# Row maxima of a banded attention: the mask moves from VectorE's add-and-max into a product on TensorE

## The chip, the cores and the metric

The kernel runs on one core of one Trainium2 chip. The metric is device time of one execution in microseconds (us), the lower the better. The median of three runs of the kernel before is 436.84 us (435.81 to 437.22).

## The reference

Three layers follow each other. The first is attention over 4 batches of 8 heads, 576 positions, head size 64, with a causal window of 128 positions and a linear bias for each head:

```python
scores = scale * np.matmul(q, k.transpose(0, 1, 3, 2))
bias = slopes[:, None, None] * (-np.abs(rel).astype(np.float32))[None, :, :]
mask = (rel >= 0) & (rel < window)
scores = np.where(mask, scores + bias[None], -1000000000.0)
scores = scores - np.max(scores, axis=-1, keepdims=True)
attn = np.exp(scores)
attn = attn / (np.sum(attn, axis=-1, keepdims=True) + 1e-09)
return np.matmul(attn, v).astype(np.float32)
```

The second is a soft mixture of 8 experts on the 2304 x 512 result (logits against `phi`, softmax over tokens to fill 32 slots, two expert products, softmax over slots to read them back). The third is a feed-forward layer, 512 to 2048 to 512, with a leaky maximum between. All of it is float32. The change touches the row maximum of the first layer alone.

## The kernel before

The first part of the kernel, up to about 160 us, is a software pipeline over the 32 heads (`g`). Each head is cut into steps with a letter each (table `UNITS`), each letter has a due time in units of heads (table `XO`), and all steps of all heads are sorted by head number plus due time and written out in that order. Engines work through their own instructions strictly in the order in which they are written, so this table sets which step stands before which on each engine; the change doesn't touch it.

The steps that matter here, for one head:

- TQ and TK: TensorE transposes q and k (L266, three instructions each, tile `tp`). HQ and HK: ScalarE rounds them into `qb` and `kb` (L279). LQ and LK: VectorE takes what the rounding left over into `kq` (L284, L286, two instructions each). DQ and DK: GpSimd copies into the other half of `kq` (L292).
- A, B, C (function `smax`): TensorE computes the scores that the row maximum is taken of, into PSUM tiles `sm`, of which there are two. The 576 rows are five tiles of 128 (the last of 64). A row tile needs the columns of its own tile and of the one before: 256, 128 for the first tile, 192 for the last. A makes tiles 0 and 1, C tiles 2 and 3, B tile 4; B stands before A. One product for a tile (L306).
- XA, XB, XC (function `smax_v`): VectorE adds the band mask `maskt` to a tile and takes the maximum of each row, in one custom instruction for a tile (L316), which also writes the sum to a scratch tile `junk`; a short second instruction then writes the maximum to a column of `mn`.
- M, MS, DM: TensorE transposes `mn` (L325), ScalarE copies it (L330, tile `ms`), and a DMA puts it as one more row into `qb` (L333), so that the next score product subtracts the maximum.
- S and s (L351, L352, tile `st`): the scores proper: two products for each of five key blocks; E0, E1: ScalarE's exponential (L359); G0, G1: GpSimd sets to zero what lies outside the band (L367 to L377); P, Q: TensorE multiplies with v (L416, 32 small products, tile `o_ps`); N1, N2, N3: VectorE divides by the row sum (L431, L433, L437).

After each eight heads a batch is complete, and its part of the mixture layer (L460 to L639: transposes, logits, maxima, slot sums) is slotted between the heads that follow. The weights of the experts stream in through SyncE's DMA queue all the while. From about 173 us on TensorE runs through the experts and the feed-forward layer almost without a break.

Set-up work stands ahead of the pipeline: GpSimd builds `maskt` from a memset with two selections (L212 to L214), after that it fills rows of `qb` and `kb` (L224, L226).

Of the kernel before, what the change touches and what calls it, by code (L numbers as in the profile page):

```python
# [13 lines left out]
ALU = mybir.AluOpType  # L14
AX = mybir.AxisListType
# [6 lines left out]
def attn_softmoe_ffn(ctx: ExitStack, tc: tile.TileContext, q, k, v, phi, w1, w2, w_in, w_out, cst_in, out):  # L22
    nc = tc.nc
    B, H, S, D = q.shape
# [32 lines left out]
    NEG = -1.0e30  # L57
# [9 lines left out]
    small = ctx.enter_context(tc.tile_pool(name="small", bufs=4))  # L67

    ident = const.tile([128, 128], F32, name="ident")
# [24 lines left out]
    def view(nm, w=None, o=0):  # L94
        w = dict(sizes)[nm] - o if w is None else w
        return ar[:, off[nm] + o:off[nm] + o + w]

    def slot(nm, dt=F32):
        if nm[0] == "a":
            t = ar[:, SLOT * int(nm[1:]):SLOT * int(nm[1:]) + SLOT]  # L100
            return t if dt == F32 else t.bitcast(dt)
        return pools[nm[0]].tile([128, SLOT], dt, tag=nm, name=nm)

    maskt = view("maskt", 256)
    units_w = [(0, g, kc, h) for h in range(2) for g in range(E // 4) for kc in range(KD)]
    units_w += [(1, g, fc, 0) for h in range(2) for g in range(E // 4) for fc in range(4 * h, 4 * h + 4)]
    W = {u: [None] * 4 for u in units_w}
# [6 lines left out]
    def put_w(i, j0, t):  # L114
        n = t.shape[1] // 512
        for j in range(n):
            W[units_w[i]][j0 + j] = t[:, 512 * j:512 * j + 512]
        return t.rearrange("p (e f) -> p e f", e=n), src_w(i, j0, j0 + n)

    with tc.manual_schedule():  # L120
# [17 lines left out]
        mn = [at.tile([128, 5], F32, name=f"mn{i}") for i in range(2)]  # L138
# [58 lines left out]
        o, i, _, _ = bulk.pop()  # L197
# [11 lines left out]
        nc.vector.memset(bm4, 1.0)  # L209
        nc.gpsimd.affine_select(out=bm4, in_=bm4, pattern=[[-32, 4], [0, 16]], compare_op=ALU.is_ge, fill=0.0, base=0, channel_multiplier=1)  # L210
        nc.gpsimd.affine_select(out=bm4, in_=bm4, pattern=[[32, 4], [0, 16]], compare_op=ALU.is_ge, fill=0.0, base=31, channel_multiplier=-1)
        nc.vector.memset(maskt, 0.0)  # L212
        nc.gpsimd.affine_select(out=maskt, in_=maskt, pattern=[[-1, 256]], compare_op=ALU.is_ge, fill=NEG, base=128, channel_multiplier=1)
        nc.gpsimd.affine_select(out=maskt, in_=maskt, pattern=[[1, 256]], compare_op=ALU.is_gt, fill=NEG, base=0, channel_multiplier=-1)  # L214
        nc.vector.reduce_sum(out=cn[:, 0, 0, :], in_=ident.rearrange("p (i c) -> p c i", c=32), axis=AX.X)
        nc.vector.tensor_copy(blk.bitcast(F32R).rearrange("p (i c) -> p i c", c=32), cn[:, 0, 0:1, :].to_broadcast([128, 4, 32]))
        nc.vector.memset(lsb[64:128, 4, :], NEG)
# [18 lines left out]
        for i in range(NP):  # L236
            t = slot(f"p{i}")
# [57 lines left out]
        sms = {}  # L295

        def smax(part):
            def f(g):
                K1, Q1 = kb[g % R], qb[g % R]
                tl = ps.tile([128, 512], F32, tag="sm", name="sm", bufs=5 - TPB)  # L300
                o, jobs = 0, []
                for t in ((0, 1), (2, 3), (4,))[part]:
                    c0, c1 = max(0, 128 * t - 128), min(S, 128 * t + 128)
                    n, mr = c1 - c0, min(128, S - 128 * t)
                    sl = tl[0:mr, o:o + n]
                    nc.tensor.matmul(sl, lhsT=Q1[:, 128 * t:128 * t + mr], rhs=K1[:, c0:c1], start=True, stop=True)  # L306
                    jobs.append((t, sl, c0 - (128 * t - 128), n, mr))
                    o += n
                sms[part, g] = jobs
            return f  # L310

        def smax_v(part):
            def f(g):
                for t, sl, m0, n, mr in sms.pop((part, g)):
                    jk = small.tile([128, 256], mybir.dt.bfloat16, tag="junk", name="junk", bufs=2)
                    nc.vector.tensor_tensor_reduce(  # L316
                        out=jk[0:mr, 0:n], in0=sl, in1=maskt[0:mr, m0:m0 + n], op0=ALU.add, op1=ALU.max,
                        accum_out=mn[g % 2][0:mr, t:t + 1], scale=1.0, scalar=NEG)
            return f

        mss = {}
# [511 lines left out]
        for h in range(2):  # L833
            pp = ps.tile([128, 512], F32, tag=f"pb{h}", name="pb")
            for g in range(2):
                for kc in range(KD):
                    t = W.pop((0, g, kc, h))
                    for j in range(4):
                        nc.tensor.matmul(pp[32 * j:32 * j + 32, :], lhsT=siT[:, g, kc, :], rhs=t[j],  # L839
                                         start=(g == kc == 0), stop=(g == 1 and kc == KD - 1), tile_position=(0, 32 * j))  # L840
                    if (h, g, kc) == (0, 0, 2):
                        p = ps.tile([128, 2], F32, tag="pa", name="pa")
# [7 lines left out]
        i, j = divmod(late + NL, 4)  # L850
        k = 0
        while i < len(units_w):
            if i == len(units_w) - PRE:
                load_wi(0, "p8")
            o, src = put_w(i, j, slot(f"p{k}")[:, 0:512 * (4 - j)])
            nc.sync.dma_start(out=o, in_=src)
            i, j, k = i + 1, 0, k + 1
# [29 lines left out]
        for i in range(2 * FC):  # L887
            _, g, fc, _ = u = units_w[2 * FC + i]
            t = W.pop(u)
            for j in range(4):  # L890
                nc.tensor.matmul(p2[32 * j:32 * j + 32, :], lhsT=hT[:, g, fc, :], rhs=t[j],  # L891
                                 start=(i == 0), stop=(i == 2 * FC - 1), tile_position=(0, 32 * j))
# [85 lines left out]
        base = 0  # L978
        for j, (t0, n, f0, f1) in enumerate(visits):
# [3 lines left out]
            base = (base + 3 * (n // TB)) % 6  # L983
# [67 lines left out]
        for n, u in enumerate(units):  # L1051
            o = n + min(1.9 + .13 * n, ZO["O"])
# [99 lines left out]
```

## Time and profile before

| what | value |
|---|---|
| median of three runs | 436.84 us |
| span of the profiled execution | 434.6 us |
| TensorE products, busy | 419.8 us, 97%, 3480 instructions |
| VectorE, busy | 284.1 us, 65%, 894 instructions |
| ScalarE, busy | 239.0 us, 55% |
| GpSimd, busy | 140.5 us, 32% |
| L316, the add-and-max (160) | 53.6 us on VectorE, 374 ns each |
| L306, its score products (160) | 34.6 us on TensorE, 310 ns each |

The profile shows one execution. The end of a product on TensorE is modelled and products overlap, so a busy share of 97% doesn't say that TensorE has no room; how far apart the starts of products stand says more, and most of the rows below are read that way. A share of the whole span also hides that VectorE is nearly always busy in the first 153 us and idle most of the time after 240 us. [...]

### The profile page before, as it was taken

The numbers are of one execution on the slowest core, as the hardware profiler recorded it, in microseconds if no ns is written. First come the engines' busy times: TensorE is split into PE (matmuls) and PEld (weight loads), VectorE is DVE, ScalarE is ACT, GpSimd is POOL, SyncE is SP. The second block draws the span as 40 slices with busy tenths as digits, with TensorE's granted clock in tenths as the row PEclk, the third lists the DMA queues.
The fourth block names the chain that finished last, engine by engine and source line by source line (L and its number), as shares of the span: only waits on it lengthen the run. The fifth ranks groups of instructions, "written<-read, shape, count | busy, mean of one in ns | idle before, by whom it ended". The sixth has DMA issues, their size and how long they took to land.

```text
span 434.6 us, 9853 instructions
## 1 busy us (share of the span) xinstructions
PE 419.8 (97%) x3480; PEld 338.2 (78%) x3480; DVE 284.1 (65%) x894; ACT 239.0 (55%) x555; POOL 140.5 (32%) x331
## 2 busy tenths in 40 slices
PE   7898999999999999999999999999999999999996
PEld 6797889888788886333877888788878888888885
DVE  7898899999999964112999885767552233225242
ACT  4586777677678733021886765555554344344440
POOL 6497788687778845020000002020202000000000
PEclk9999999999999999999999999999999999999999
DMA  7768777778867979999987005000000003004012
GB/s 163 222 185 230 227 221 215 219 207 243 229 197 220 261 254 391 321 407 413 411 305 245 31 2 193 2 1 0 2 0 0 2 9 137 0 0 148 0 74 72
DMA packets 66801, 70.15 MB, mean 161 GB/s; under 512 B 23168, under 2 KB 42016, under 8 KB 66752
## 3 DMA queue, kind: packets, MB, share of 16 engines
q1 hardware_dynamic: 66304, 69.24, 49.5%
q8 instruction: 28, 0.46, 0.4%
q10 hardware_dynamic: 448, 0.28, 0.2%
q14 instruction: 21, 0.17, 0.1%
HBM read 64.70 MB, written 4.72 MB: 160 GB/s over the span
## 4 chain that ended last, share of the span: by engine, by line
PE 84%; DVE 6%; DMA 5%; issue 2%; POOL 1%; ACT 1%; DVEq 0%; SPq 0%; POOLq 0%; ACTq 0%
PE acc L1015 45%; PE o_ps L416 6%; PE ph L992 4%; PE sm L306 4%; PE pb L839 3%; PE pb L891 3%; PE st L352 3%; PE st L351 3%; PE tp L266 3%; DMA qb<-ms 2%; DMA ar<-in_q_dram 2%; DVE kq L284 1%; DMA ar<-in_k_dram 1%; PE tp L460 1%; PE tp L482 1%
## 5 line engine op out<-in xcount | busy, mean ns | idle before, releaser
L1015 PE MATMUL acc<-p,p 128*128 128x512 f32 x648 | 158.7, 390 | 0.0
L1015 PEld LDWEIGHTS acc<-p,p 128*128 128x128 f32 x648 | 120.7, 188 | 24.5 <-issue 1.7
L1005 DVE TENSOR_TENSOR p<-ar,p 128x384 fp32r<-128x384 f32 x96 | 52.9, 556 | 89.6 <-ACT ar L1001 89.4
L997 ACT ACTIVATE p<-ph 128x384 fp32r<-128x384 f32 (+1 forms) x97 | 47.5, 491 | 92.4 <-PE ph L992 92.4
L316 DVE CUSTOM_DVE_ANT_0 junk<-sm,ar 128x256 bf16<-128x256 f32 (+2 forms) x160 | 53.6, 374 | 4.5 <-PE sm L306 4.1
L1015 PE MATMUL acc<-b,p 128*128 128x512 f32 x216 | 53.6, 392 | 0.0
L785 POOL TENSOR_TENSOR p<-ar,p 128x512 fp32r<-128x512 f32 x8 | 10.6, 1329 | 124.9 <-ACT p L785 108.7
L359 ACT ACTIVATE ar<-st 128x512 f32<-128x512 f32 x64 | 38.3, 599 | 17.2 <-PE st L352 9.8
L1001 ACT ACTIVATE ar<-ph 128x384 f32<-128x384 f32 x96 | 47.1, 490 | 0.0
L1015 PEld LDWEIGHTS acc<-b,p 128*128 128x128 f32 x216 | 40.1, 188 | 8.2 <-DVE ql L1030 0.4
L416 PE MATMUL o_ps<-ar 128*64 128x65 f32 x992 | 41.3, 227 | 0.0
L416 PEld LDWEIGHTS o_ps<-ar 128*64 128x64 f32 x992 | 36.5, 137 | 4.7 <-issue 1.0
L351 PE MATMUL st<-kq 128*128 128x256 f32 (+1 forms) x160 | 39.7, 277 | 0.0
L352 PE MATMUL st<-qb,kb 128*128 128x256 f32 (+1 forms) x160 | 35.7, 270 | 2.1 <-DMA qb<-ms 2.1
L306 PE MATMUL sm<-kb,qb 128*128 128x256 f32 (+2 forms) x160 | 34.6, 310 | 2.6 <-DVE mn L316 1.0
L279 ACT ACTIVATE qb<-tp 64x288 fp32r<-64x288 f32 x64 | 28.0, 437 | 14.0 <-PE tp L266 13.2
L992 PE MATMUL ph<-p,p 128*128 128x384 f32 x96 | 33.1, 350 | 0.0
L266 PE MATMUL tp<-ident,ar 96*128 96x96 f32 x192 | 28.5, 258 | 2.3 <-DMA ar<-in_q_dram 1.4
L352 PEld LDWEIGHTS st<-qb,kb 128*128 128x128 f32 (+1 forms) x160 | 28.6, 179 | 2.5 <-DMA qb<-ms 2.5
L284 DVE SCALAR_TENSOR_TENSOR kq<-tp,qb 64x288 fp32r<-64x288 f32 x64 | 29.2, 457 | 1.9
L279 ACT ACTIVATE kb<-tp 64x288 fp32r<-64x288 f32 x64 | 28.0, 437 | 4.4 <-PE tp L266 3.0
L286 DVE TENSOR_TENSOR kq<-tp,kb 64x288 fp32r<-64x288 f32 x64 | 29.1, 454 | 1.7
(204 smaller groups left out, 618.0 us busy)
## 6 DMA issues: line engine op xcount, KB each, us to landing
p<-in_moe_w_dram SPq DMA_DIRECT2D x56, 256.0 KB
p<-in_moe_w_dram SPq DMA_DIRECT2D x7, 1024.0 KB
p<-in_moe_w_in_dram SPq DMA_DIRECT2D x5, 1024.0 KB
p<-in_moe_w_out_dram SPq DMA_DIRECT2D x5, 1024.0 KB
ar<-in_q_dram SPq DMA_DIRECT2D x32, 144.0 KB
ar<-in_k_dram SPq DMA_DIRECT2D x31, 144.0 KB
out_dram<-ar SPq DMA_DIRECT2D x17, 256.0 KB
ar<-in_v_dram SPq DMA_DIRECT2D x32, 128.0 KB
```

The source lines that it names most:

```text
L266: nc.tensor.transpose(p[:, 96 * u:96 * u + 96], n[:, 128 * u:128 * u + 128], ident[0:96, 0:96])
L279: nc.scalar.activation(out=b1, in_=pr, func=AF.Copy, scale=2.0 ** (g % H - 2) if half else 1.0)
L306: nc.tensor.matmul(sl, lhsT=Q1[:, 128 * t:128 * t + mr], rhs=K1[:, c0:c1], start=True, stop=True)
L316: nc.vector.tensor_tensor_reduce(out=jk[0:mr, 0:n], in0=sl, in1=maskt[0:mr, m0:m0 + n], op0=ALU.add, op1=ALU.max, accum_out=mn[g % 2][0:mr ...
L351: nc.tensor.matmul(sl, lhsT=KX[:, k0:k1], rhs=QA[:, q0:q1], start=True, stop=False)
L352: nc.tensor.matmul(sl, lhsT=kb[g % R][:, k0:k1], rhs=qb[g % R][:, q0:q1], start=False, stop=True)
L416: nc.tensor.matmul(o_ps[64 * u:64 * u + 64, t, :], lhsT=lt, rhs=r, start=st, stop=sp, tile_position=(0, 64 * u))
L992: nc.tensor.matmul(p, lhsT=mst[:, 128 * f:128 * f + 128], rhs=rhs, start=True, stop=True)
L997: nc.scalar.activation(out=G[t0, f][0][:, c], in_=H1[t0, f][:, c], func=AF.Prelu, alpha=0.01)
L1001: nc.scalar.activation(out=gg, in_=H1.pop((t0, f)), func=AF.Prelu, alpha=0.01)
L1005: nc.vector.tensor_tensor(out=g2, in0=G0.pop((t0, f)), in1=g1.bitcast(F32), op=ALU.subtract)
L1015: nc.tensor.matmul(acc[t0][t], lhsT=(g1, g1, g2)[k][:, 128 * t:128 * t + 128], rhs=(WO1, WO2, WO1)[k][c][:, i], start=(f == f0 and k == 0) ...
```

## The change

The mask becomes a bfloat16 tile of 320 columns, and a bfloat16 copy `idb` of the unit matrix stands beside it in the same place in SBUF. In `smax`, each score product is preceded by a product of `idb` with a piece of the mask into the same piece of PSUM; the score product then adds onto it. The tiles are grouped anew: A makes tiles 1 and 2, C tiles 3 and 4, both 256 columns wide (tile 4 is now taken with 128 rows, of which 64 are padding, and 256 columns), and B makes tile 0 with 128 columns. In `smax_v`, VectorE takes the plain maximum (`reduce_max`) of both tiles of A in one instruction, the same for C, and of the one tile of B. The scratch tile `junk` is gone.

```diff
-    maskt = view("maskt", 256)
+    BF16 = mybir.dt.bfloat16
+    maskt = view("maskt", 160).bitcast(BF16)
+    idb = view("maskt", 64, 160).bitcast(BF16)
...
+        nc.vector.tensor_copy(idb, ident)
         nc.vector.memset(maskt, 0.0)
-        nc.gpsimd.affine_select(out=maskt, in_=maskt, pattern=[[-1, 256]], compare_op=ALU.is_ge, fill=NEG, base=128, channel_multiplier=1)
-        nc.gpsimd.affine_select(out=maskt, in_=maskt, pattern=[[1, 256]], compare_op=ALU.is_gt, fill=NEG, base=0, channel_multiplier=-1)
+        nc.gpsimd.affine_select(out=maskt, in_=maskt, pattern=[[-1, 320]], compare_op=ALU.is_ge, fill=NEG, base=192, channel_multiplier=1)
+        nc.gpsimd.affine_select(out=maskt, in_=maskt, pattern=[[1, 320]], compare_op=ALU.is_gt, fill=NEG, base=-64, channel_multiplier=-1)
...
-                for t in ((0, 1), (2, 3), (4,))[part]:
-                    c0, c1 = max(0, 128 * t - 128), min(S, 128 * t + 128)
-                    n, mr = c1 - c0, min(128, S - 128 * t)
-                    sl = tl[0:mr, o:o + n]
-                    nc.tensor.matmul(sl, lhsT=Q1[:, 128 * t:128 * t + mr], rhs=K1[:, c0:c1], start=True, stop=True)
+                ts = ((1, 2), (3, 4), (0,))[part]
+                w = 256 if part < 2 else 128
+                for i, t in enumerate(ts):
+                    c1 = min(S, 128 * t + 128)
+                    m0 = 64 + 256 - w + c1 - (128 * t + 128)
+                    nc.tensor.matmul(tl[:, w * i:w * i + w], lhsT=idb, rhs=maskt[:, m0:m0 + w], start=True, stop=False)
+                    nc.tensor.matmul(tl[:, w * i:w * i + w], lhsT=Q1[:, 128 * t:128 * t + 128], rhs=K1[:, c1 - w:c1], start=False, stop=True)
...
-                for t, sl, m0, n, mr in sms.pop((part, g)):
-                    jk = small.tile([128, 256], mybir.dt.bfloat16, tag="junk", name="junk", bufs=2)
-                    nc.vector.tensor_tensor_reduce(
-                        out=jk[0:mr, 0:n], in0=sl, in1=maskt[0:mr, m0:m0 + n], op0=ALU.add, op1=ALU.max,
-                        accum_out=mn[g % 2][0:mr, t:t + 1], scale=1.0, scalar=NEG)
+                t, sl = sms.pop((part, g))
+                nc.vector.reduce_max(out=mn[g % 2][:, t:t + sl.shape[1]], in_=sl, axis=AX.X)
```

On TensorE, the stretch of one head from the end of its products with v (`o_ps`) to the start of the scores proper (`st`) holds the maxima's transpose and then B and A. Before:

```order
L416 MATMUL o_ps<-ar 64x65 x16
L325 MATMUL tp<-ident,mn_98 5x128
L306 MATMUL sm<-kb_94,qb_95 64x192
L306 MATMUL sm<-kb_94,qb_95 128x128
L306 MATMUL sm<-kb_94,qb_95 128x256
L351 MATMUL st<-kq_90 128x256
```

The same place now (lines are a few numbers off; `ar` is the place in SBUF that holds `idb` and the mask, and the loading of `idb` has a row of its own):

```order
L415 MATMUL o_ps<-ar 64x65 x16
L324 MATMUL tp<-ident,mn_98 5x128
L309 LDWEIGHTS ar
L309 MATMUL sm<-ar 128x128
L310 MATMUL sm<-kb_94,qb_95 128x128
L309 LDWEIGHTS ar
```

Three score products of 192, 128 and 256 columns have become six products, of 128, 128 and four times 256 columns; C, a little later, goes from two products of 256 columns to four.

On VectorE, the stretch of one head from the division of a head's result (N1: L431) to the leftover of the next q (LQ: L284) holds XB, XA and XC. Before:

```order
L431 TENSOR_SCALAR rs<-o_ps 128x5
L316 ISA junk,mn_98<-sm,ar 64x192
L316 ISA mn_98 64x1
L433 RECIPROCAL rs<-rs 128x5
L437 TENSOR_TENSOR ar<-o_ps,rs 128x5x64
L316 ISA junk,mn_98<-sm,ar 128x128
L316 ISA mn_98 128x1
L316 ISA junk,mn_98<-sm,ar 128x256
```

After the last row its short second instruction follows, and then the same pair twice more, for C. The same place now:

```order
L430 TENSOR_SCALAR rs<-o_ps 128x5
L317 TENSOR_REDUCE mn_98<-sm 128x1
L432 RECIPROCAL rs<-rs 128x5
L436 TENSOR_TENSOR ar<-o_ps,rs 128x5x64
L317 TENSOR_REDUCE mn_98<-sm 128x2 x2
L287 SCALAR_TENSOR_TENSOR kq_96<-tp,qb_95 64x288 x2
```

Ten instructions of a head have become three; their places among the others are the same, and what follows them is the same.

## Rows read from the trace of the kernel before

**Rows 1.** Stretch: length, busy PE, PEld, DVE, ACT, POOL (instructions), clock, DMA share, GB/s
```profile
59.45:97.69 38.24, 37.03 (x520) 32.63 (x518) 36.15 (x153) 28.02 (x69) 29.83 (x74) 1.00 0.77 216
```

**Rows 2.** VectorE in order of time, one head: start, us, engine, line, operation, shapes
```profile
91.53 0.49 DVE L437 TENSOR_TENSOR ar<-o_ps,rs 128x320 f32<-128x320 f32 x1
91.94 0.28 DVE L316 CUSTOM_DVE_ANT_0 junk<-sm,ar 128x128 bf16<-128x128 f32 x1
...
92.14 0.42 DVE L316 CUSTOM_DVE_ANT_0 junk<-sm,ar 128x256 bf16<-128x256 f32 x1
...
93.29 0.95 DVE L284 SCALAR_TENSOR_TENSOR kq<-tp,qb 64x288 fp32r<-64x288 f32 x2
...
95.33 0.34 DVE L316 CUSTOM_DVE_ANT_0 junk<-sm,ar 64x192 bf16<-64x192 f32 x1
...
95.60 0.17 DVE L433 RECIPROCAL rs<-rs 128x5 f32<-128x5 f32 x1
95.81 0.49 DVE L437 TENSOR_TENSOR ar<-o_ps,rs 128x320 f32<-128x320 f32 x1
```

**Rows 3.** TensorE in order of time, one head with batch work, 117.96 to 122.61 us
```profile
117.96 0.27 PE L325 MATMUL tp<-ident,mn 128*5 128x128 f32 x1
117.99 0.58 PE L306 MATMUL sm<-kb,qb 128*64 128x192 f32 x3
118.41 0.28 PE L351 MATMUL st<-kq 128*128 128x256 f32 x1
118.53 0.28 PE L352 MATMUL st<-qb,kb 128*128 128x256 f32 x1
...
118.89 0.28 PE L630 MATMUL tp<-col,dn 128*128 128x2 f32 x2
...
119.42 0.36 PE L351 MATMUL st<-kq 128*128 128x256 f32 x1
...
120.07 0.66 PE L460 MATMUL tp<-ident,ar 128*128 128x128 f32 x4
120.56 0.41 PE L266 MATMUL tp<-ident,ar 96*128 96x96 f32 x3
120.76 0.48 PE L306 MATMUL sm<-kb,qb 128*128 128x256 f32 x2
121.07 0.41 PE L266 MATMUL tp<-ident,ar 96*128 96x96 f32 x3
121.42 1.26 PE L416 MATMUL o_ps<-ar 128*64 128x65 f32 x32
122.61 0.27 PE L325 MATMUL tp<-ident,mn 128*5 128x128 f32 x1
```

**Rows 4.** TensorE by line and shape, 59.45 to 97.69 us: busy, mean ns | idle before
```profile
L460 PE MATMUL tp<-ident,ar 128*128 128x128 f32 x16 | 2.5, 279 | 0.0
...
L482 PE MATMUL tp<-ar,phi_sb 128*32 128x144 f32 x32 | 1.4, 292 | 0.0
```

**Rows 5.** VectorE by line and shape, same stretch: busy, mean ns | idle before, releaser
```profile
L316 DVE CUSTOM_DVE_ANT_0 junk<-sm,ar 128x256 bf16<-128x256 f32 x24 | 9.0, 417 | 0.5 <-PE sm L306 0.5
...
L622 DVE COPY SI<-tp 128x512 f32<-128x512 f32 x1 | 0.7, 691 | 0.0
...
L562 DVE TENSOR_REDUCE cm<-lsb 128x5 f32<-128x160 f32 x1 | 0.3, 271 | 0.0
...
L538 DVE TENSOR_REDUCE mx<-tp 128x32 f32<-128x128 f32 x1 | 0.2, 244 | 0.0
```

**Rows 6.** Listed waits of TensorE, same stretch: who for whom, total us, times, longest
```profile
PE tp L266 <- DVE mn L316: 0.7, 1, 0.7
```

**Rows 7.** Set-up, in order of time: VectorE's cast and GpSimd's first mask selection
```profile
4.63 0.26 DVE L216 CAST blk<-cn 128x128 fp32r<-128x128 f32 x1
...
4.77 0.40 POOL L213 TENSOR_SCALAR_AFFINE_SELECT ar<-ar 128x256 f32<-128x256 f32 x1
```

**Rows 8.** Chain of work that ended last: the longest DMA piece of the maxima
```profile
32.54 5.38 DMA qb<-ms
```

More of the change, by code (lines that the diff above doesn't have):

```diff
@@ L300, in f @@
                 tl = ps.tile([128, 512], F32, tag="sm", name="sm", bufs=5 - TPB)
-                o, jobs = 0, []
-                for t in ((0, 1), (2, 3), (4,))[part]:
-                    c0, c1 = max(0, 128 * t - 128), min(S, 128 * t + 128)
-                    n, mr = c1 - c0, min(128, S - 128 * t)
-                    sl = tl[0:mr, o:o + n]
-                    nc.tensor.matmul(sl, lhsT=Q1[:, 128 * t:128 * t + mr], rhs=K1[:, c0:c1], start=True, stop=True)
-                    jobs.append((t, sl, c0 - (128 * t - 128), n, mr))
-                    o += n
-                sms[part, g] = jobs
+                ts = ((1, 2), (3, 4), (0,))[part]
[5 more added lines that the diff above has]
+                    nc.tensor.matmul(tl[:, w * i:w * i + w], lhsT=Q1[:, 128 * t:128 * t + 128], rhs=K1[:, c1 - w:c1], start=False, stop=True)
+                sms[part, g] = ts[0], tl[:, 0:w * len(ts)].rearrange("p (t c) -> p t c", c=w)
             return f
```

## The prediction

> **What bounds the kernel now.** I read the stretch of the page where the changed lines run, the heads up to about 153 us, and nothing behind it: TensorE's experts and feed-forward part issue the same work afterwards and only start earlier or later. The first view to read is the busy time by stretch. From 59.45 to 97.69 us lie eight heads, 38.24 us, with one whole set of batch work: VectorE is busy 36.15 us of it, TensorE 37.03, GpSimd 29.8, ScalarE 28.0 [rows 1]. Two engines look full, so the order of time has to tell which one is.
>
> VectorE is. In a head without batch work its instructions stand nose to tail: from the start of N3 to the next N3 it is 91.53 to 95.81, 4.28 us, and every instruction starts before or right after the one ahead of it has ended [rows 2]. The only listed idle time ahead of a group in the eight heads is 0.5 us, once [rows 5].
>
> TensorE only looks full, since modelled ends overlap the next start. Its starts tell what it needs. In the head from 117.96 to 122.61 us it runs through 4.65 us with no wait that I can see [rows 3]. Of that, batch work is what stands between 118.89 and 119.42 us, and the four transposes of L460 from 120.07 to 120.56, together 1.02. So a bare head takes TensorE 3.63 us, say 3.6. Eight of them are 28.8. The batch work of eight heads I put at 5.5 us: 16 transposes at about 0.12 (0.49 for four in rows 3) make 2.0, the 32 logit products 1.4 by their busy time [rows 4], and the slot sums and small products, about as many, an estimated 2.1. TensorE therefore needs about 34.3 of the 38.24 us and has 3.9 us to spare, 0.49 us a head. One of its stalls on VectorE's maxima is listed by name, 0.7 us [rows 6].
>
> **What the change takes from VectorE.** XB, XA and XC cost from start to next start: XB 95.33 to 95.60, 0.27; XA and XC 91.94 to 93.29, 1.35; together 1.62 us a head [rows 2]. Three plain maxima take their place, one over 128 and two over 512 elements a row. The trace has maxima over 128 elements in PSUM, 244 ns, and over 160, 271 ns, but none over 512 [rows 5]. By the slope of the add-and-max, whose 128 and 256 element forms last 0.28 and 0.42 us [rows 2], 384 more elements cost about 0.42, so 512 last 0.66 us. A plain copy of 512 elements out of PSUM lasts 0.691 [rows 5], which fits. On this engine the next start comes about 0.08 us before the end (N3 lasts 0.49, the next starts after 0.41 [rows 2]), so the three cost 0.17 + 2 x 0.58 = 1.33. The second instruction that fetches each maximum goes, too. VectorE saves 0.29 us a head; at worst, with no overlap and the copy's duration, 0.24 + 2 x 0.69 = 1.62 and it saves nothing. I take 0.29, since every pair in these rows overlaps.
>
> [...]
>
> **What the change adds to TensorE.** Five mask products a head, and wider score products. A 256-wide product starts 0.12 us after the one ahead (118.41, 118.53), with weights of its own each time [rows 3]. C is now two such products from 120.76 to 121.07, 0.31; four of them make 0.48: +0.17. B and A take 117.99 to 118.41, 0.42 [rows 3]; the new A is 0.48, and the new B, two products of 128 columns, I put at 0.17 (one at 0.12, the four transposes' price, one at about 0.05, half of a 256-wide one, if the load of `idb` is short): +0.23. Together +0.40 us a head, 3.2 for eight. No row shows a bfloat16 weight load. From below, some products may run while TensorE would wait anyway, for the two `sm` tiles or for `kb` and `qb`, and cost nothing. From above, all ten products take 0.12 whatever their width, and what the present five take over that (0.73 - 5 x 0.12 = 0.13) stays: 1.33 against 0.73, +0.60. I take 0.40, as the 256-wide products are the larger part and their price is a row.
>
> [...]
>
> **Other edits.** Set-up gains a cast of 128 columns on VectorE, 0.26, and GpSimd's two selections grow from 256 to 320 columns, 0.40 to about 0.50 each [rows 7]; the first score products wait for what GpSimd does right behind. I count +0.25, all on the path. SyncE's queue gets nothing new. The DMA of the maxima (M, MS, DM) keeps its place; it sits behind weight transfers, and where one took 5.38 us it set the end of a chain [rows 8]. That stall stays whatever the engines save. The mask products wait for a free `sm` tile as the score products did; behind a waiting one stand C and the next transposes, as now. Since B's maximum comes out sooner (0.17 against 0.27), that wait does not grow.
>
> **The sum.** For eight heads VectorE now needs 38.24 - 8 x 0.29 = 35.9 and TensorE 34.3 + 3.2 = 37.5: the bound changes hands. I leave 0.4 us of waits with TensorE (the maxima's DMA, GpSimd's masks), 37.9, so eight heads lose 0.3 us. The stretch from the first batch work (about 36 us) to the last maxima (about 153) is 117 / 38.24 = 3.06 such sets: -0.9. Ahead of it stand about three bare heads of 4.28; they come down to TensorE's 3.6 + 0.40 = 4.0: -0.85. Set-up +0.25. In all -1.5 us on a span of 434.6, which is 433.1. The median of the runs stands 2.2 above that span (436.84 - 434.6), so 435.3 us.
>
> **Rivals.**
> One: VectorE stays the bound, because the new products fall into TensorE's waits. Eight heads would take 35.9: 3.06 x -2.3 - 0.85 + 0.25 = -7.6, 429.2 us. For it speaks the wait in rows 6 and that TensorE's bare head has waits of its own behind VectorE; against it, that rows 3 holds no wait and is nearly all products.
> Two, the slower side: the mask products cost TensorE more than it has to spare. The point is 0.44 us a head, where 34.3 + 0.4 + 8 x 0.44 reaches 38.24. At 0.55, between my two ends, it is 39.1 for eight heads, 3.06 x 0.86 = +2.6, bare heads 4.15, -0.4, set-up +0.25: +2.5, 439.3 us. For it speaks that each score product must load 128 columns of weights behind a product that may be as short as 128 columns; against it, the steady 0.12.
> Two b: no load is hidden. Each mask product then costs its 0.12 twice, +1.0 us a head, about 451 us. The 0.12 of rows 3 is against it.
> Three, the change doesn't do what it says: a maximum over two tiles is no cheaper than two add-and-max. Eight heads stay at 38.24, TensorE's 37.5 is hidden under it, set-up stays: 437.1 us. The 0.691 copy in rows 5 allows it if overlap fails.
>
> **How the numbers follow.** My forecast gets 0.46, one 0.15, two 0.25, two b 0.02, three 0.12. What a measurement of this kernel can tell from no change is about 0.3%, 1.3 us, and the forecast sits just beyond that edge: of its 0.46 I count 0.25 as faster, 0.19 as no change, 0.02 as slower. Faster: 0.25 + 0.15 = 0.40. Within: 0.19 + 0.11 (three) = 0.30. Slower: 0.02 + 0.25 + 0.02 + 0.01 = 0.30. For the range, one reaches down to 429.2 and two up to 440.7 at the upper price of 0.60 (34.3 + 4.8 + 0.4 = 39.5, 3.06 x 1.26 - 0.24 + 0.25 = +3.9). I cut both ends a little and give 430.5 to 440.0; what lies outside is half of one, a quarter of two, and two b, under 0.2. The forecast's own range is 433 to 437.
>
> **What would show it.** On VectorE, L317 with 512 elements at about 0.66 us and the next start 0.08 earlier; three of them 1.33 us a head. On TensorE, C as four products from 0.45 to 0.50 us and B with A at about 0.65. VectorE should show idle time behind TensorE's `sm` or `o_ps` in most heads, a bare head should take 4.0 us and eight heads about 37.9. Eight heads near 36 mean rival one, over 38.5 rival two, L317 near 0.7 with no overlap rival three. I would be wrong altogether if the stretch after 170 us changed its length, for instance because weights come too late for heads that end sooner.

## The result, and the profile after

The kernel after takes 441.59 us (median of four runs, 440.35 to 442.64), the kernel before 436.32 in the same comparison (four runs). The ratio is 1.013, with a 95% interval from 1.010 to 1.016: slower by 1.3%, where 435.3 us was forecast. The profiled execution spans 439.7 us, against 434.6 before, so 5.1 us have to be found. The start of N3, which every head has once on VectorE, cuts the span into stretches (us):

| stretch | before | after | difference |
|---|---|---|---|
| start to the first N3 | 25.47 | 27.49 | +2.0 |
| first to ninth N3 | 36.23 | 36.22 | 0 |
| ninth to 17th | 38.38 | 39.22 | +0.8 |
| 17th to 25th | 38.33 | 39.48 | +1.2 |
| 25th to the end | 296.2 | 297.3 | +1.1 |

Behind the heads nothing changed: from the last N3 in the profile to the end it is 270.7 us in both. The loss lies in the start and in the heads.

The first view is again the busy time by stretch, here for the two sets of eight heads from one maxima transpose to the one eight later (columns as in [rows 1], which it answers):

```profile
61.81:101.09 39.28, 39.28 (x559) 35.46 (x557) 36.35 (x97) 27.75 (x68) 29.71 (x74) 1.00 0.76 216
101.09:140.58 39.49, 39.45 (x559) 35.52 (x558) 36.71 (x98) 27.80 (x69) 29.64 (x74) 1.00 0.74 211
```

TensorE, which has 39 instructions more, now has no gap left in the first of them (39.28 of 39.28, by the modelled ends), and eight heads take 39.3 to 39.5 us instead of 38.24. VectorE is as busy as it was (36.35 against 36.15) with 97 instructions in place of 153. The count fell, the time did not.

TensorE in order of time, the head that answers [rows 3] (same place in the program, start, us, engine, line, operation, shapes):

```profile
121.48 0.27 PE L324 MATMUL tp<-ident,mn 128*5 128x128 f32 x1
121.59 0.22 PE L309 MATMUL sm<-ar 128*128 128x128 bf16 x1
121.62 0.31 PE L310 MATMUL sm<-kb,qb 128*128 128x128 f32 x1
121.76 0.29 PE L309 MATMUL sm<-ar 128*128 128x256 bf16 x1
121.81 0.36 PE L310 MATMUL sm<-kb,qb 128*128 128x256 f32 x1
122.01 0.28 PE L309 MATMUL sm<-ar 128*128 128x256 bf16 x1
122.05 0.36 PE L310 MATMUL sm<-kb,qb 128*128 128x256 f32 x1
122.25 0.28 PE L350 MATMUL st<-kq 128*128 128x256 f32 x1
...
124.40 0.41 PE L269 MATMUL tp<-ident,ar 96*128 96x96 f32 x3
124.65 0.28 PE L309 MATMUL sm<-ar 128*128 128x256 bf16 x1
...
125.13 0.41 PE L269 MATMUL tp<-ident,ar 96*128 96x96 f32 x3
...
126.67 0.28 PE L324 MATMUL tp<-ident,mn 128*5 128x128 f32 x1
```

The head takes 5.19 us, against 4.65 in [rows 3]: +0.54, and three places hold all of it. From the maxima's transpose to the scores (`st`) it is 0.77 instead of 0.45, +0.32; the transposes ahead of C take 0.25 instead of 0.20, +0.05; C takes 0.48 instead of 0.31, +0.17. What stands elsewhere in the head is 3.69 us in both.

VectorE, one head without batch work (answers [rows 2]):

```profile
98.74 0.49 DVE L436 TENSOR_TENSOR ar<-o_ps,rs 128x320 f32<-128x320 f32 x1
99.15 1.30 DVE L317 TENSOR_REDUCE mn<-sm 128x2 f32<-128x512 f32 x2
100.48 0.95 DVE L287 SCALAR_TENSOR_TENSOR kq<-tp,qb 64x288 fp32r<-64x288 f32 x2
...
102.51 0.28 DVE L317 TENSOR_REDUCE mn<-sm 128x1 f32<-128x128 f32 x1
102.71 0.18 DVE L432 RECIPROCAL rs<-rs 128x5 f32<-128x5 f32 x1
102.93 0.49 DVE L436 TENSOR_TENSOR ar<-o_ps,rs 128x320 f32<-128x320 f32 x1
```

The two paired maxima take 1.33 us from start to next start, the single one 0.20, and the head 4.19 against 4.28. By line and shape, busy and mean ns (answers [rows 5]):

```profile
L317 DVE TENSOR_REDUCE mn<-sm 128x2 f32<-128x512 f32 x16 | 10.8, 685 | 1.3 <-PE sm L310 1.2
...
L317 DVE TENSOR_REDUCE mn<-sm 128x1 f32<-128x128 f32 x8 | 2.2, 280 | 0.0
```

And who waits for whom from 25 to 165 us (total, times, longest), first before, then after:

```profile
PEld st L352 <- DMA qb<-ms: 2.5, 2, 1.5
...
DVE junk L316 <- PE sm L306: 2.0, 4, 0.9
```

```profile
DVE mn L317 <- PE sm L310: 6.7, 13, 1.3
...
PEld st L351 <- DMA qb<-ms: 0.2, 1, 0.2
```

VectorE now waits for TensorE's scores, 6.7 us in place of 2.0. The listed wait for the maxima's DMA has gone from 2.5 us to 0.2; in the other five traces with at least five mask products a head it is 0 to 0.5. What the slower pipeline has to do with it is not shown: e4 below, as slow as this kernel, still has 2.0.

### The profile page after: what moved, and what is told of

Read it like the earlier page. It is cut to its first block, busy times and chain, and to the rows that moved or that the text cites. A ratio compares the mean times of both kernels' runs of the same rounds, so it can differ in the third digit from the quotient of the medians.

```text
span 439.7 us, 9856 instructions
## 1 busy us (share of the span) xinstructions
PE 431.6 (98%) x3640; PEld 350.9 (80%) x3640; DVE 283.2 (64%) x671; ACT 238.5 (54%) x555; POOL 140.3 (32%) x331
## 4 chain that ended last, share of the span: by engine, by line
PE 95%; DMA 1%; DVE 1%; ACT 1%; issue 0%; POOL 0%; DVEq 0%; SPq 0%; ACTq 0%
PE acc L1014 45%; PE o_ps L415 8%; PE sm L310 5%; PE ph L991 4%; PE tp L269 4%; PE sm L309 4%; PE st L351 4%; PE st L350 4%; PE pb L838 3%; PE pb L890 3%; PE tp L459 2%; PE tp L324 1%; PE o_ps L154 1%; PE tp L481 1%; PE tp L611 1%; PE ph L941 1%
## 5 line engine op out<-in xcount | busy, mean ns | idle before, releaser
L317 DVE TENSOR_REDUCE mn<-sm 128x2 f32<-128x512 f32 (+1 forms) x96 | 51.7, 550 | 10.3 <-PE sm L310 10.0
L358 ACT ACTIVATE ar<-st 128x512 f32<-128x512 f32 x64 | 38.3, 598 | 22.9 <-PE st L351 11.5
L310 PE MATMUL sm<-kb,qb 128*128 128x256 f32 (+1 forms) x160 | 46.4, 358 | 1.0 <-ACT kb L282 1.0
L309 PE MATMUL sm<-ar 128*128 128x256 bf16 (+1 forms) x160 | 40.4, 272 | 0.2 <-DVE mn L317 0.2
L415 PE MATMUL o_ps<-ar 128*64 128x65 f32 x992 | 39.2, 225 | 0.0
L415 PEld LDWEIGHTS o_ps<-ar 128*64 128x64 f32 x992 | 34.8, 138 | 4.1 <-POOL ar L376 0.7
L282 ACT ACTIVATE qb<-tp 64x288 fp32r<-64x288 f32 x64 | 27.7, 433 | 13.5 <-PE tp L269 12.8
L310 PEld LDWEIGHTS sm<-kb,qb 128*128 128x128 f32 x160 | 31.7, 200 | 3.9 <-issue 1.5
L287 DVE SCALAR_TENSOR_TENSOR kq<-tp,qb 64x288 fp32r<-64x288 f32 x64 | 29.3, 457 | 1.8
```

What stands on the lines that cost most here:

```text
L282: nc.scalar.activation(out=b1, in_=pr, func=AF.Copy, scale=2.0 ** (g % H - 2) if half else 1.0)
L309: nc.tensor.matmul(tl[:, w * i:w * i + w], lhsT=idb, rhs=maskt[:, m0:m0 + w], start=True, stop=False)
L310: nc.tensor.matmul(tl[:, w * i:w * i + w], lhsT=Q1[:, 128 * t:128 * t + 128], rhs=K1[:, c1 - w:c1], start=False, stop=True)
L317: nc.vector.reduce_max(out=mn[g % 2][:, t:t + sl.shape[1]], in_=sl, axis=AX.X)
L415: nc.tensor.matmul(o_ps[64 * u:64 * u + 64, t, :], lhsT=lt, rhs=r, start=st, stop=sp, tile_position=(0, 64 * u))
```

## The experiments

All ratios are to the kernel before, run beside them on the same chip. The edits are shown shortened. The theory at the outset: TensorE's added work is more than it has to spare. The rival: the paired maxima are the loss, because a pair's maximum comes only when both tiles are there.

**Without mask products** (e1):

```diff
-   nc.tensor.matmul(tl[...], lhsT=idb, rhs=maskt[:, m0:m0 + w], start=True, stop=False)
-   nc.tensor.matmul(tl[...], lhsT=Q1[...], rhs=K1[...], start=False, stop=True)
+   nc.tensor.matmul(tl[...], lhsT=Q1[...], rhs=K1[...], start=True, stop=True)
```

> The kernel after without the five mask products of a head; VectorE's plain maxima of two tiles stay. The maxima are then taken over unmasked columns, so this kernel computes something else than the reference. Theory (TensorE's added products are the loss): TensorE falls back to about 34.5 us for eight heads, VectorE is the bound again at about 36, bare heads near 4.0, and the time is 428 to 431 us, some 12 below the kernel after. Rival (the paired maxima themselves are the loss: a pair's maximum comes out only when both tiles are done, so the maxima's transpose comes later): the time stays within 2 us of the kernel after, about 441.

It took 435.13 us, ratio 0.9996 (0.9985 to 1.0008). The loss is gone, so the paired maxima are not the loss. But neither is there a gain that can be measured, even with the mask for nothing: theory and rival both missed the time. The bare head on VectorE:

```profile
90.55 0.49 DVE L435 TENSOR_TENSOR ar<-o_ps,rs 128x320 f32<-128x320 f32 x1
90.96 1.28 DVE L316 TENSOR_REDUCE mn<-sm 128x2 f32<-128x512 f32 x2
92.27 0.95 DVE L287 SCALAR_TENSOR_TENSOR kq<-tp,qb 64x288 fp32r<-64x288 f32 x2
...
94.71 0.49 DVE L435 TENSOR_TENSOR ar<-o_ps,rs 128x320 f32<-128x320 f32 x1
```

VectorE stands nose to tail at 4.16 us: it wins 0.12 us a head, not the 0.29 of the prediction. The ninth to the 17th N3 take 37.70 us (38.38 before), but the 17th to the 25th 38.55. Only the bare heads get shorter. Three heads with batch work in a row take 4.64, 5.06 and 4.44 us on TensorE from one maxima transpose to the next (78.87 to 93.01 us), against 4.64, 5.00 and 4.38 in the kernel before (79.67 to 93.69): relieving VectorE does nothing for them, so it was not what bound them.

**Mask products and the old add-and-max** (e2): the products of the kernel after, and for each tile the custom instruction of the kernel before.

```diff
-   nc.vector.reduce_max(out=mn[g % 2][:, t:t + sl.shape[1]], in_=sl, axis=AX.X)
+   for t, sl, m0, n in sms.pop((part, g)):
+       nc.vector.tensor_tensor_reduce(out=jk[:, 0:n], in0=sl, in1=maskt[:, m0:m0 + n],
+           op0=ALU.add, op1=ALU.max, accum_out=mn[g % 2][:, t:t + 1], ...)
```

> The kernel after with its mask products, but VectorE takes the maxima as before, one add-and-max for each tile (the mask is added twice, which leaves the maxima as they are). Theory (TensorE sets the time): about the kernel after or a little slower, 441 to 444 us, since VectorE at 38.2 to 38.4 us for eight heads stays under TensorE's 39.4. Rival (the paired maxima are the loss): back to about 437.

441.28 us, ratio 1.0136 (1.0116 to 1.0156): the kernel after's ratio again, with the old VectorE work. Eight heads (columns as above):

```profile
60.57:100.03 39.46, 39.34 (x559) 35.50 (x557) 37.35 (x153) 27.83 (x68) 29.75 (x74) 1.00 0.75 215
```

Together with e1 this settles the sides: the mask products make the whole loss, and the paired maxima change nothing that can be measured.

**Each mask product twice** (e10): does TensorE still have anything to spare?

```diff
+   nc.tensor.matmul(tl[...], lhsT=idb, rhs=maskt[:, m0:m0 + w], start=False, stop=False)
```

> The kernel after with each mask product issued twice, which adds the mask twice and leaves the maxima as they are: five more products a head, each behind its twin, with the same weights. Theory (TensorE is the bound in the kernel after, so nothing more is hidden): + 4 x 0.12 + 0.07 = 0.55 us a head, times 31 heads in the pipeline = 17, some 458 us. Rival (TensorE still has a share of waits to fill, VectorE bounds the heads without batch work): half of it, 447 to 451.

453.77 us, ratio 1.041 (1.037 to 1.045), 12.4 us above the 441.3 of the other runs with five products, between the two expectations. The trace tells why:

```profile
60.71:103.53 42.82, 42.82 (x600) 39.04 (x599) 36.58 (x97) 27.76 (x68) 29.78 (x74) 1.00 0.71 195
```

Eight heads take 42.82 us, 3.5 more than in the kernel after, all of them TensorE's; a bare head takes 4.61 instead of 4.17, so five twins cost 0.44 and not 0.55: 0.09 us each on average, less than I had put for a product with the weights of the one ahead. 12.4 is 28 times 0.44, nearly all of the heads. So TensorE was the bound already, and the expectation's mechanism held, at a lower price.

**Score product first** (e3):

```diff
-   nc.tensor.matmul(tl[...], lhsT=idb, rhs=maskt[:, m0:m0 + w], start=True, stop=False)
-   nc.tensor.matmul(tl[...], lhsT=Q1[...], rhs=K1[...], start=False, stop=True)
+   nc.tensor.matmul(tl[...], lhsT=Q1[...], rhs=K1[...], start=True, stop=False)
+   nc.tensor.matmul(tl[...], lhsT=idb, rhs=maskt[:, m0:m0 + w], start=False, stop=True)
```

> The kernel after with the two products of each tile in the other order: the score product opens the tile, the mask product adds onto it. Nothing else changes. Theory (part of the loss is the load of the unit matrix in the open, 0.08 us behind the maxima's transpose and 0.05 behind the transposes ahead of C): both gaps close, 0.13 us a head over some 32 heads, so 437.5 to 439.5 us. Rival (the gap belongs to the change of type or of work, not to the place of the load): the gaps appear between other products and the time stays at 441 to 442.

443.80 us, ratio 1.019 (1.016 to 1.021), 2.5 us above e2 on the same chip: slower still, so the theory of the uncovered load fell. TensorE, around B and A:

```profile
103.21 0.27 PE L324 MATMUL tp<-ident,mn 128*5 128x128 f32 x1
103.24 0.30 PE L309 MATMUL sm<-kb,qb 128*128 128x128 f32 x1
...
103.43 0.36 PE L309 MATMUL sm<-kb,qb 128*128 128x256 f32 x1
103.64 0.28 PE L310 MATMUL sm<-ar 128*128 128x256 bf16 x1
103.67 0.36 PE L309 MATMUL sm<-kb,qb 128*128 128x256 f32 x1
103.88 0.28 PE L310 MATMUL sm<-ar 128*128 128x256 bf16 x1
103.92 0.36 PE L350 MATMUL st<-kq 128*128 128x256 f32 x1
104.12 0.28 PE L351 MATMUL st<-qb,kb 128*128 128x256 f32 x1
```

The gap behind the maxima's transpose closes (0.03), and another opens: the first product of the scores is followed only after 0.20 us instead of 0.12. C with its transposes takes 0.82 instead of 0.78 in a head without batch work. So the gap goes with the change from one kind of product to another, not with the place of one load; the types alone don't make it, for the kernel before has the same 0.20 between score products behind a batch's transposes (119.42 in [rows 3], next start 119.62).

**Fewer mask columns** (e4, e11). e4 masks only the 128 columns of a tile's own positions, by one product for a pair; e11 does so tile by tile, in the order of e3.

```diff
 e4:
+   mk = maskt.rearrange("p (t c) -> p t c", c=128)[:, ...]
+   tv = tl[:, 0:w * len(ts)].rearrange("p (t c) -> p t c", c=w)[:, :, w - 128:w]
+   nc.tensor.matmul(tv, lhsT=idb, rhs=mk, start=False, stop=True)
 e11:
+   nc.tensor.matmul(tl[:, w * i + w - 128:w * i + w], lhsT=idb, rhs=maskt[:, m0 + w - 128:m0 + w], start=False, stop=True)
```

> Fewer mask columns: only the 128 columns of a row tile's own positions are masked (positions ahead in the window are left in the maximum, which may only raise it), by one product of 256 columns for a pair of tiles and one of 128 for the single tile, each behind its score products. Three mask products a head instead of five, 640 columns instead of 1152. Theory (TensorE's added time a head against the 0.44 it has to spare decides): about +0.12 for each pair and +0.08 for the single tile, +0.32 in place of +0.53; TensorE then needs 34.3 + 0.4 + 8 x 0.32 = 37.3 us for eight heads, VectorE 35.9; 432 to 435 us, plus up to 1.8 if the slower start-up belongs to the change. Rival (each product costs its place whatever its width, or the maxima are the loss): 438 to 441.

> Score product first, then a mask product of 128 columns over the row tile's own positions alone, for each tile: the order of the run with the score product first, with four of the five mask products half as wide. Positions ahead in the window are left in the maximum, which may only raise it. Theory (a product costs by its columns): 4 x 0.05 = 0.2 us a head less than with the score product first, 31 heads: 443.8 - 6.2 = 437.5 to 439. Rival (a product behind a load costs 0.12 whatever its width): 443 to 444.

e4: 441.31 us, ratio 1.013 (1.011 to 1.014): three mask products a head, and no faster than five. In the head that answers [rows 3], 121.22 to 126.21 us, it takes TensorE 4.99 us, +0.34, about as reckoned; but the ninth to the 17th N3 still take 40.0 us, with a wait of 1.5 us for the maxima's DMA among them, and the 17th to the 25th 38.9. e11: 445.37, ratio 1.020 (1.017 to 1.023), above both expectations; the same head takes 5.19 us, against 5.24 in e3 with masks twice as wide:

```profile
124.36 0.36 PE L309 MATMUL sm<-kb,qb 128*128 128x256 f32 x1
124.56 0.23 PE L310 MATMUL sm<-ar 128*128 128x128 bf16 x1
124.61 0.36 PE L309 MATMUL sm<-kb,qb 128*128 128x256 f32 x1
```

A score product and a mask product take 0.25 us together with 128 mask columns (124.36 to 124.61), and 0.24 to 0.25 with 256 in the same order (103.43 to 103.92 in e3). That is e11's rival, and the first half of e4's: the width of the mask product isn't the price.

**One pair alone** (e9): tiles 1 and 2 as in the kernel after, tiles 0, 3 and 4 as before.

```diff
+   if part:   # tiles 3 and 4, tile 0: one product, add-and-max, as before
+       nc.tensor.matmul(sl, lhsT=Q1[...], rhs=K1[:, c0:c1], start=True, stop=True)
```

> The change for one pair of tiles alone: tiles 1 and 2 get mask products and one plain maximum, tiles 0, 3 and 4 keep the kernel before's single product and VectorE's add-and-max. Theory (break-even: what TensorE gets more is free up to about 0.44 us a head, behind VectorE's 4.28): two mask products cost 0.24 to 0.3 us a head, no loss; VectorE gains 0.05 to 0.08 a head of the two-tile maximum; 434 to 436.5 us, the same as the kernel before within 0.4%. Rival (each product costs its 0.12 us, as TensorE is full in any case): 2 x 0.12 x 31 heads = 7 us more at worst, by the share of the kernel after (5.3 us for 0.53) 438 to 439.

438.54 us, ratio 1.0046 (1.0024 to 1.0068, 12 runs against 17). In the head of [rows 3] TensorE needs only 0.18 us more (118.93 to 123.76 us, 4.83), far less than the 0.44 that I had called free, and yet the kernel is slower. Its waits, 25 to 165 us:

```profile
PEld sm L311 <- ACT kb L282: 1.5, 6, 0.4
```

The wait is no longer than in the kernel before (1.7, 6, 0.4), so it is not itself the loss; it shows a loop. TensorE stands still behind the maxima's transpose until ScalarE has rounded k for B, and that k came from TensorE's own transposes. One head of this kind, first in the kernel before, then here: the first product of B, the next transposes of q, the next maxima transpose.

```profile
123.09 0.56 PE L306 MATMUL sm<-kb,qb 128*64 128x192 f32 x3 [0.20 <-ACT kb L279]
...
125.33 0.47 PE L266 MATMUL tp<-ident,ar 96*128 96x96 f32 x3
...
127.61 0.27 PE L325 MATMUL tp<-ident,mn 128*5 128x128 f32 x1
```

```profile
124.27 0.33 PE L311 MATMUL sm<-kb,qb 128*128 128x128 f32 x1 [0.23 <-ACT kb L282]
...
126.78 0.47 PE L269 MATMUL tp<-ident,ar 96*128 96x96 f32 x3
...
129.06 0.28 PE L342 MATMUL tp<-ident,mn 128*5 128x128 f32 x1
```

From B to the transposes of q it is 2.24 us before and 2.51 here: the two mask products of A stand in this stretch and come out in full. From there to the next maxima transpose it is 2.28 in both, and only 2.31 in the kernel after, although C has two mask products more there: they fill time in which TensorE waited. So four heads in a row, three of them with this wait, take 0.9 us more than before (79.61 to 98.52 against 79.67 to 97.69 us; eight heads later it is 0.9 again), with idle time left on TensorE. A mean over eight heads counts that idle time as room. The three traces agree in this, but no run changed the loop alone. Of the 1.9 us by which the profiled span is longer, 0.8 lie ahead of the first N3.

**The start** (e5, e6): one more warm-up product ahead of the first transposes, in the kernel before and in the kernel after.

```diff
-    WN = [5, 1, 0, 2, 3, 0, 0]
+    WN = [6, 1, 0, 2, 3, 0, 0]
```

> The kernel before with six warm-up products ahead of the first transposes instead of five, so that TensorE works on to about 4.4 us and cannot stand idle before q has landed (3.9 to 4.2 us in the profiles so far). Theory (in the profiles where TensorE was idle 0.2 us ahead of its first transposes its products ran at half speed until about 10.5 to 11.5 us, and where it was not, until about 5 to 6 us; the break decides): full speed by 6 us, first N3 within 25.2 to 25.9 us, and the time 0 to 1 us below the kernel before, with less spread. Rival (an idle 0.2 us has nothing to do with it): products at half speed past 9 us in spite of the longer warm-up.

> The kernel after with the same sixth warm-up product. Theory (1.3 of the 2.0 us that the profiled kernel after is late at the first N3 are the break ahead of the first transposes, the rest the change): first N3 at 26.0 to 26.6 us in place of 27.5, the time about 440.5 us, and 3.5 to 5 us above the kernel before with the same warm-up. Rival (the late start belongs to the mask's set-up and products): first N3 stays at 27.2 to 27.7 and the time at 441.5.

e5: 436.64 us, ratio 0.999 (0.996 to 1.002), first N3 at 26.03. e6: 441.32 us, ratio 1.012 (1.009 to 1.015), first N3 at 26.14. In the profiled kernel after the products ran at half their later pace until 10.4 us (from three transposes to the next product it is 0.48 us at 8.89, 0.25 at 10.85); in e6 until 6.3. The clock column shows 1.00 from the start to 14 us all the same, so that it is the clock is not shown. TensorE in order of time, three rows of each, first the kernel after (what stood idle ahead of a row is in brackets):

```profile
4.12 0.74 PE L269 MATMUL tp<-ident,ar 96*128 96x96 f32 x3 [0.19 <-DMA ar<-in_q_dram]
...
9.37 0.69 PE L154 MATMUL o_ps<-ident 128*128 128x128 f32 x2
...
10.63 0.38 PE L154 MATMUL o_ps<-ident 128*128 128x128 f32 x2
```

```profile
4.15 0.69 PE L269 MATMUL tp<-ident,ar 96*128 96x96 f32 x3
...
5.59 0.69 PE L154 MATMUL o_ps<-ident 128*128 128x128 f32 x2
...
6.92 0.43 PE L154 MATMUL o_ps<-ident 128*128 128x128 f32 x2
```

So of the 2.0 us at the first N3, 1.35 go with the late full pace in that one execution. What is left with an early pace is 0.1 against e5 and 0.7 against the kernel before (26.14 against 26.03 and 25.47). Without mask products a late pace costs less: the first N3 comes at 25.55, 25.74 and 26.22 in e13, e1 and e12, with half pace until 10.1, 11.5 and 13.1 us. So a part of the 1.35 comes only with the mask products on TensorE. That the idle 0.2 us ahead of the first transposes decides the pace is not shown: e9 and e10 had that idle time and full pace by 6.8 and 5.5 us, e8 and e13 had none and got it at 9.8 and 10.1. It differs from execution to execution, and the medians of e6 and of the kernel after hardly differ. What sets it stays open.

**Where VectorE's 0.12 us went** (e7, e8, e12, e13). First the maxima's DMA was moved away from the weight transfers, without mask products (e7) and in the kernel before (e8):

```diff
-            nc.sync.dma_start(out=qb[g % R][MROW:MROW + 1, :]...
+            nc.scalar.dma_start(out=qb[g % R][MROW:MROW + 1, :]...
```

> The kernel after without its mask products (maxima over unmasked columns, so it computes something else than the reference), and with the DMA of the maxima issued from ScalarE's queue instead of SyncE's, where it stands behind weight transfers. Theory (VectorE's 0.12 us a head went into waits of the score products for that DMA, 2.2 us in the profile, and for k, 1.0): these waits fall under 0.5 us and the time to 431 to 433 us. Rival (the gain is missing for another reason: TensorE is the bound in the heads with batch work): 434.5 to 435.5 as with SyncE's queue.

> The kernel before with the DMA of the maxima issued from ScalarE's queue. Theory (2.1 to 2.5 us of waits for it in the profile, part of them covered by VectorE, which is the bound): 434 to 435 us, about 1 to 2 below the kernel before. Rival (all covered, or the transfer takes as long from any queue): no change, or slower by the issue on ScalarE.

e7: 441.03 us, ratio 1.013 (1.008 to 1.018); e8: 442.33, ratio 1.016 (1.009 to 1.023). Both are slower, which neither theory had, though e8's rival allowed it; the waits for that DMA stay (2.9 and 2.7 us of weight loads on `qb<-ms`, 25 to 165 us), with up to 2.0 us at a time before the first N3, which comes at 28.06 and 29.59. From there to the last N3 e8 takes as long as the kernel before (138.5 us); its loss lies in the start. Another queue did not make this transfer come sooner, so these two runs don't answer the question. The second attempt sends fewer weights in the heads:

```diff
-   issue(n + x, (1 if n < 0 else (1.25, 1)[n % 2] if n < 24 else ...
+   issue(n + x, (1 if n < 0 else (.75, .75)[n % 2] if n < 24 else ...
```

> The kernel after without its mask products (maxima over unmasked columns, so it computes something else than the reference), and with the experts' weights sent at three quarters of a piece for each of three places in a head, instead of 1 to 1.25, in the first 24 heads; what is left is sent behind the heads, so the experts may wait for it, and only the heads are read. Theory (VectorE's 0.12 us a head went into waits for the maxima's DMA and for k behind weight transfers): those waits fall under 0.7 us, every bare head takes 4.16, and first N3 to the N3 of the 25th head takes at most 110 us, in place of 111.7 without products at the full pace and 112.9 in the kernel before. Rival (TensorE's batch work bounds the other heads): 111 us or more with the waits gone.

> The kernel before with the same slower sending of weights. Theory: its waits for the maxima's DMA, 2.1 us of TensorE, fall under 0.7; VectorE is the bound in every head, so first N3 to the N3 of the 25th head goes from 112.9 us to about 111.5, and the gap to the run without products at the same pace is 24 x 0.07 to 24 x 0.12 = 1.7 to 2.9 us. Rival: 112.5 or more, the waits were covered, and the gap is under 1 us, as at the full pace.

The whole kernels take 443.42 and 444.77 us (ratios 1.017 and 1.020, two runs each), as the experts then wait for weights. From the first N3 to the 25th:

| | full pace | slower weights |
|---|---|---|
| kernel before | 112.9 us | 110.9 us (e13) |
| without mask products | 111.7 us | 109.7 us (e12) |

TensorE's waits for DMA, 25 to 137 us, without products at full pace, and then with slower weights:

```profile
PE st L350 <- DMA qb<-ms: 1.6, 3, 1.0
...
PE tp L269 <- DMA ar<-in_k_dram: 1.0, 1, 1.0
```

```profile
PE tp L269 <- DMA ar<-in_q_dram: 0.2, 1, 0.2
```

With slower weights no wait for the maxima's DMA is listed any more in this stretch, and none in e13 either (2.1 us in the kernel before). Both kernels take 2.0 us less, and without products the time to the 25th N3 fell under 110, as the theory had it. But the gap between the two stays 1.2 us, 0.05 a head, between the two expectations. Fifteen of the 24 heads are 0.11 to 0.12 us shorter without products, the other nine together 0.5 us longer (the head from 69.85 us takes 5.73 without products, and the one from 69.83 us 5.28 in the kernel before): more than half of VectorE's 0.12 a head is lost in the longer heads, those with batch work, not to the DMA. At full pace the last N3 of e1 comes 0.6 us earlier than in the kernel before (163.4 against 163.95); the medians show nothing of it, and executions of one kernel differ by more.

## Why the prediction was wrong, point by point

- **What bounds the kernel now: right for bare heads alone.** There VectorE is the bound (4.28 us, and 4.16 as soon as its work shrinks). I read that from one bare head and took it for all; the heads with batch work don't get shorter when VectorE is relieved (e1), so in them it was not. TensorE's need of 34.3 us for eight heads was too low, too. The kernel after needs 39.3 with hardly anything idle, five products cost 0.54 a head, so without them it is 39.3 - 8 x 0.54 = 35.0. The batch work is not what was short: by the starts in the stretch from 61.81 us it takes 5.3 us (5.5 in the sum), 2.3 of them for the small products that I had put at 2.1. What is left is 3.7 us for a head, short waits included, in place of 3.6.
- **What TensorE gets: the first step that failed.** I had +0.40 a head; it is +0.54. C (+0.17) and the products of B and A (0.66 against a forecast of 0.65) came out as reckoned. What I left out is 0.13 us where the work changes: 0.08 between the maxima's transpose and the first mask product, 0.05 between the transposes and C. With base and price as measured the sum reads 35.0 + 4.3 = 39.3 (the base was taken from that total, so this is no check), in place of 34.3 + 3.2 + 0.4 = 37.9; 1.4 us for eight heads over 3.06 sets are 4.3 of the 6.3 us that the forecast was off.
- **The spare time: the second step that failed.** I divided 3.9 us by eight and called 0.44 us a head free. e9 adds 0.18 and loses 2 us. e4 adds 0.34 and loses as much as the kernel after, though a wait for the maxima's DMA has a part in that. Heads differ (in the kernel after 4.17 us for a bare one, 6.34 for the longest, 115.14 to 121.48), and part of the idle time is a wait inside a loop through TensorE and ScalarE, where added work is nearly free behind the transposes of q (0.03 us) and paid in full ahead of them (0.27).
- **What VectorE saves: 0.12 us, not 0.29.** The maxima last 0.685 us (forecast 0.66). I let each overlap the next instruction by 0.08; the first of the two does (0.60), but the second is followed by L287, which starts 0.03 after its end. The same tail stood in the 1.35 of [rows 2], and I had dropped it from the new side alone. Measured are 1.51 us a head in e1.
- **Bare heads at the start: -0.85 forecast, +0.1 seen** from the first N3 to the fourth (12.91 us against 12.82). Two of these three heads take 4.16 to 4.17, the first 4.58. With VectorE at 4.16 and TensorE at 4.11 (4.18 from 96.91 to 101.09 us, less the 0.07 by which B and A are longer there than the 0.77 above) a bare head could not reach 4.0.
- **Set-up: +0.25 forecast, +2.0 in the profile**, of which 1.35 goes with the late full pace; with six warm-up products in both kernels +0.1. GpSimd's two mask selections took 0.45 us each, in place of 0.40 [rows 7], and the cast of `idb` 0.16.
- **Rival two was the case, at its price:** 0.55 was its example, 0.54 the measurement, and its point of 0.44 was passed. It gave 439.3 us because it rested on the same 34.3. Rival one (products in TensorE's waits) fell with the first stretch shown above; rival three (a maximum over two tiles is no cheaper) was half right; rival two b (no load is hidden) was not seen: a mask and a score product of 256 columns with weights of their own take 0.24 us together.
- **Behind 170 us nothing changed**, as was assumed.

No version here that computes the reference beats the kernel before, and the mask for nothing (e1) would give no more than it has.

## What to carry to other kernels

Before work moves from a full engine to one that seems to have room, price the receiving engine's neighbours too: the gap that opens where its work changes kind was a quarter of the cost here. TensorE's mean idle time over eight heads overstated its room here (0.49 us a head by my count, and 0.18 more in e9 already cost 2 us), and in the loop through ScalarE only the stretch in which it waits had room (0.03 us of cost for C's mask products behind the transposes of q, 0.27 for A's ahead of them); adding a fraction of the change and looking at the time shows it cheaply. And price the side that is relieved by the instruction that follows: here the next start came 0.08 us before the end of the first paired maximum, and 0.03 after the end of the second.

## What was not expected of the hardware

- A bfloat16 mask product between two float32 score products costs the same at 128 and at 256 columns: with its score product of 256 columns it takes 0.24 to 0.25 us either way (e11 and e3). A second mask product right behind the first, with the same weights, costs 0.09 on average (0.44 for five, e10); the trace has a weight load for it too (599 loads in eight heads, 557 in the kernel after).
- The first float32 product behind a bfloat16 one is followed 0.20 us later, where a series of float32 products keeps 0.12; so the mixed series has starts 0.04 and 0.20 apart in turn, 0.24 for two (the kernel after).
- With the same instructions on TensorE up to there, its products go from half to full pace at about 5.8 us in the kernel before and at 10.1 in e13. Over all traces it is 4.7 (e5) to 13.5 us (e11).
- A transfer of 2.5 KB for the maxima is waited for as long from ScalarE's queue as from SyncE's (2.7 and 2.5 us from 25 to 165 us, e8 and the kernel before), and in e8 for another 2.7 us before that. So another queue was no way round the weight transfers here.
